# AV of a chunk's second query block as one 128-row matmul per head, in a fused sliding-window attention and SwiGLU kernel

## The chip, the cores and the metric

One Trainium2 chip; the kernel runs on one of its cores. The time is the device time of one execution in microseconds, given as the median of several runs.

## What is computed

```python
# q, k, v: (8, 8, 576, 64) float32;  w_gate, w_val: (512, 1536);  w_out: (1536, 512)
scores = np.matmul(q, k.transpose(0, 1, 3, 2)) / 8.0
mask = (rel >= 0) & (rel < 64)             # rel = query position - key position
attn = softmax(np.where(mask, scores, -1e9))
attn_out = np.matmul(attn, v)              # (8, 8, 576, 64)
x = attn_out.transpose(0, 2, 1, 3).reshape(4608, 512)
g = x @ w_gate
out = (g * sigmoid(g) * (x @ w_val)) @ w_out      # (4608, 512) float32
```

A query sees itself and the 63 positions before it in its own batch. The 4608 tokens are 8 batches of 576.

## The kernel before

The tokens are cut into 36 chunks of 128 (`NCH`), each of two blocks of 64 queries. A query block sees the keys of its own block and of the block before it. Four chunks make one FFN chunk of 512 tokens (`NFC` = 9).

Every step is written by hand, and `_Graph` turns its reads and writes into semaphore waits. Each engine runs its steps in exactly the order in which `build` issues them, so TensorE's order is the order of the calls. The steps that matter here:

- `S(n)` (`Sa`, `Sbias`, `Sb`): scores of chunk n, transposed (keys on partitions). Per pair of heads it issues 64x64 matmuls (lines 394 and 398). ScalarE's Exp writes `pt` (line 406), and VectorE multiplies by the mask (line 409); in the first chunks a matmul with `nmask` (line 374) adds a bias in place of the mask.
- `pt[n]` holds, for each of 8 heads, a 128x128 block. Partitions 0 to 63 are the keys of the chunk's first block, for all 128 queries. Partitions 64 to 127 hold for the first 64 columns (first query block) the keys of the *previous* chunk's last block, and for the last 64 columns (second query block) the keys of the chunk's own second block.
- `AV(n)` (`AVa`, `AVmm`, `AVn`): probabilities times V, with a column of ones in V that gives the sums. `AVmm` runs in two phases of 16 matmuls (line 439), each of 64 rows, 64 columns of weights and 65 moving columns. `r` is the row half of the TensorE array (which keys) and `c` the column half (which query block); in a phase the four matmuls of one `j` go to the four quadrants of the array. The two phases add into the same PSUM, and phase 1 waits for the end of phase 0 by a semaphore (`after=done[0]`). `AVn` divides by the sums on VectorE (lines 454, 457) into `xb`.
- `X(n)`: transposes `xb` into `xT`, by TensorE (line 490) in the first chunks, later by a DMA on SP's queue. `T2` (line 347) transposes k and q of the first chunks on TensorE with 128 rows and 64 columns of weights; later chunks use DMA transposes.
- `F(c, fs)`: gate and value matmuls of an FFN chunk, 128x128 weights and 512 moving columns (256 or 128 in places), 4 per `f` and weight (line 552), then Tanh on ScalarE (line 558) and two VectorE steps (lines 560, 562) into `hT`.
- `O(c, u)`: 12 matmuls of 128x128 weights and 512 columns (line 578), a copy on ScalarE (line 583) and a store on its queue.

`build` first loads (`loads`; on GpSimd's DMA queue, in order of issue), runs dummy matmuls on zeros (`warm`, line 527), then an opening with chunks 0 to 3 in a hand-made order, then chunks 4 to 11 mixed with the F steps of FFN chunks 0 and 1. From FFN chunk 2 on there is a regular stage for each token chunk n:

```python
self.load(n + 4)
self.B(n)          # AVmm(n, 0), S(n + 1), AVmm(n, 1), AVn(n)
self.X(n)
self.Tkq(n + 3)
F(c, (3 * u,)); F(c, (3 * u + 1,)); O(c - 1, u); F(c, (3 * u + 2,))
```

`B` is also what chunks 8 to 11 use; it puts the scores of the next chunk between the two phases of AV.

Of the kernel before, what the change touches and what calls it, by code (L numbers as in the profile page):

```python
# [151 lines left out]
class _Kernel:  # L152
# [181 lines left out]
    def T2(self, st, x, engs):  # L334
        g = self.g
        src = (self.ks2 if x == "k" else self.qs2)[st % 2]
        dst = self.kT if x == "k" else self.qT
        z0 = (2 * st) % self.NZ
        for cc in range(2):
            bank, bk = self.bank("a")  # L340
            tb = bank[:, 0:256].bitcast(BF).rearrange("p (c j t) -> p c j t", c=2, j=2)

            def pe(e, cc=cc, tb=tb):
                for c in range(2):
                    for j in range(2):
                        for p in range(2):
                            r = e.transpose(tb[64 * p:64 * p + 64, c, j, :], src[:, 4 * cc + 2 * c + p, j, :], self.ident[:, :])  # L347
                return r

            g.op("pe", pe, reads=["ident", ("s2", x, st % 2, 0), ("s2", x, st % 2, 1)], writes=[bk])  # L350
            d = dst[:, 2 * cc:2 * cc + 2, 128 * z0:128 * z0 + 256].rearrange("p c (t j) -> p c t j", j=2)
            a = tb.rearrange("p c j t -> p c t j")
            self.copy(engs[cc], d, a, [bk], [(x + "T", z, cc) for z in (z0, z0 + 1)])
# [57 lines left out]
    def S(self, n, bias=False):  # L411
        if n < NCH:
            self.Sb(self.Sa(n, bias))
# [9 lines left out]
    def AVmm(self, st, phase):  # L423
        n, bx, av, done = st
        iv, jv, ip = n % self.NV, (n - 1) % self.NV, n % self.NP
        va, vb, pt = self.va[iv], self.va[jv], self.pt[ip]

        def pe(e):
            for j in range(4):
                for r in range(2):  # L430
                    p = r if phase == 0 else 1 - r
                    h = 2 * j + p
                    for c in range(2):
                        if n == 0 and r == 1 and c == 0:
                            continue
                        first = j == 0 and (phase == 0 or (n == 0 and c == 0 and r == 0))
                        rows = slice(64 * r, 64 * r + 64)
                        vv = vb if (r == 1 and c == 0) else va
                        x = e.matmul(av[64 * c:64 * c + 64, p, j, :], pt[rows, h, 64 * c:64 * c + 64], vv[rows, h, 0:65],  # L439
                                     start=first, stop=phase == 1, skip_group_check=True)  # L440
            return x

        rd = [("pt", ip, 0), ("pt", ip, 1)]
        for i in {iv, jv} if n else {iv}:
            rd += [("va", i), ("va", i, 0), ("va", i, 1)]
        done.append(self.g.op("pe", pe, reads=rd, writes=[b[1] for b in bx], after=done[0] if phase else None))
# [27 lines left out]
    def X(self, n, eng="sp", kind="f"):  # L474
        if n >= NCH:
            return
        g = self.g
        ix, it, u = n % 4, (n // 4) % self.NX, n % 4
        xb = self.xb[ix]
        xo = self.xT[it][:, :, 128 * u:128 * u + 128]  # L480
        xk = [("xb", ix, 0), ("xb", ix, 1)]
        if eng == "sp":
            g.op("sp", lambda e: e.dma_start_transpose(xo, xb[:, :]), reads=xk, writes=[("xT", it, u)], dma=True)
            return
        bank, bk = self.bank(kind)
        tb = bank[:, 0:256].bitcast(BF).rearrange("p (c t) -> p c t", c=4)

        def pe(e):
            for c in range(4):
                r = e.transpose(tb[:, c, :], xb[:, 128 * c:128 * c + 128], self.ident[:, :])  # L490
            return r

        g.op("pe", pe, reads=["ident"] + xk, writes=[bk])
        self.copy(eng, xo, tb, [bk], [("xT", it, u)])
# [122 lines left out]
    def loads(self):  # L617
        self.first_loads()
        self.load2(0, "q")
        self.load2(1, "k")  # L620
        self.load2(1, "q")
        self.init()
        self.init_ident()
        self.init_mask(0)
        self.init_mask(1)
        self.load(0, "v")
        self.load(1, "v")
        self.load_w("g", 0, 2)
        self.load(2, "v")
        self.load(3, "v")  # L630
        self.load_w("v", 0, 2)
        for a in range(2, 10, 2):
            self.W(a, a + 2)

# [21 lines left out]
    def build(self):  # L656
        F, S, AV, X, T2, O = self.F, self.S, self.AV, self.X, self.T2, self.O
        self.loads()
        self.banks("a", [4, 5, 6, 7, 0, 1, 2, 3, 4, 5, 0, 1, 2, 3, 0, 1, 6, 7, 4, 5, 6, 7, 4, 5, 2, 3, 6, 7])
        self.warm(90, n=64)  # L660
        self.first_T(("dve", "act"))
        self.init_nmask()
        self.warm(2)
        s0 = self.Sa(0)
        T2(0, "q", ("act", "dve"))
        self.Sbias(s0)
        self.Sb(s0)
        T2(1, "k", ("dve", "dve"))
        s1 = self.Sa(1, True)
        self.Sb(s1)  # L670
        T2(1, "q", ("dve", "act"))
        self.early_loads()
        s2, s3 = self.Sa(2, True), self.Sa(3)
        a0, a1, a2, a3 = self.AVa(0), self.AVa(1), self.AVa(2), self.AVa(3)
        self.AVmm(a0, 0)
        self.AVmm(a0, 1)
        self.AVn(a0)
        self.Sb(s2)
        self.AVmm(a1, 0)
        self.AVmm(a1, 1)  # L680
        self.AVn(a1)
        self.Sbias(s3)
        X(0, "act", "a")
        self.Sb(s3)
        X(1, "dve", "a")
        self.AVmm(a2, 0)
        self.AVmm(a2, 1)
        self.AVn(a2)
        self.AVmm(a3, 0)
        self.AVmm(a3, 1)  # L690
        self.AVn(a3)
        F(0, (0, 1), 0, 256)
        X(2, "act", "a")
        X(3, "act", "a")
        F(0, (2, 3), 0, 256)
        F(0, (0, 1), 256, 512)
        self.banks("a", [4, 5, 6, 7])
        self.init_va(4, self.NV)
        self.more_loads()
        F(0, (2, 3), 256, 512)  # L700
        F(0, (4, 5), 0, 256)
        F(0, (4, 5), 256, 512)
        F(0, (6, 7), 0, 256)
        F(0, (6, 7), 256, 512)
        T2(2, "k", ("act", "act"))
        T2(2, "q", ("act", "act"))
        F(0, (8, 9), 0, 256)
        S(4)
        F(0, (8, 9), 256, 512)
        S(5)  # L710
        AV(4)
        F(0, (10,), 0, 512)
        AV(5)
        F(0, (11,))
        X(4, "act")
        T2(3, "k", ("act", "act"))
        X(5, "act")
        F(1, (0, 1), 0, 128)
        T2(3, "q", ("act", "act"))
        F(1, (0, 1), 128, 256)  # L720
        S(6)
        F(1, (2, 3), 0, 256)
        S(7)
        AV(6)
        F(1, (4, 5), 0, 256)
        AV(7)
        F(1, (6, 7), 0, 256)
        X(6, "act")
        F(1, (8, 9), 0, 256)
        X(7, "act")  # L730
        for n in (10, 11, 12):
            self.load(n)
        for n in range(8, 12):
            self.Tkq(n)
        F(1, (10, 11), 0, 256)
        S(8)
        F(1, (0, 1), 256, 512)
        O(0, 0)
        self.load(13)
        self.load(14)  # L740
        self.Tkq(12)
        self.B(8)
        X(8)
        self.Tkq(13)
        F(1, (2, 3), 256, 512)
        O(0, 1)
        self.load(15)
        self.B(9)
        X(9)
        self.Tkq(14)  # L750
        F(1, (4, 5), 256, 512)
        F(1, (6, 7), 256, 512)
        self.B(10)
        O(0, 2)
        F(1, (8, 9), 256, 512)
        X(10, "act")
        self.B(11)
        O(0, 3)
        F(1, (10, 11), 256, 512)
        X(11, "act")  # L760
        for c in range(2, NFC):
            for u in range(4):
                n = 4 * c + u + 4
                if n < NCH:
                    self.load(n + 4)
                    self.B(n)
                    self.X(n)
                    self.Tkq(n + 3)
                F(c, (3 * u,))
                F(c, (3 * u + 1,))  # L770
                if n < NCH or u < 3:
                    O(c - 1, u)
                F(c, (3 * u + 2,))
                if n >= NCH and u == 3:
                    O(c - 1, u)
        for u in range(3):
            O(NFC - 1, u)
        self.O_last(NFC - 1, 3)
        self.g.emit()
# [42 lines left out]
```

## Time and profile before

| | us |
|---|---|
| median of 3 runs (lowest, highest) | 338.50 (337.32, 338.95) |
| the profiled execution, its own time | 337.56 |
| its span, first to last instruction | 335.7 |
| TensorE matmuls busy, by the page | 321.4 (96%) |
| VectorE busy | 202.1 (60%) |
| ScalarE busy | 136.2 (41%) |
| GpSimd busy | 105.9 (32%) |

Matmuls overlap in TensorE, so the mean duration of a matmul in the profile is its latency, not the distance to the next one; the distance comes from the starts of neighbouring records. PEld is the loading of weights, with a record of its own for each matmul. Some matmul records are missing from the trace, regularly the first gate matmul after an AV.

### The profile page before, as it was taken

What the parts mean: (1) busy time and instruction counts of PE and PEld (TensorE: products, weight loads), DVE (VectorE), ACT (ScalarE), POOL (GpSimd) and SP (SyncE); (2) the same over time, 40 slices, a digit from 0 to 9 for tenths busy, and PEclk for the clock granted to TensorE, in tenths of its full rate; (3) what the DMA queues carried; (4) which work ended last, traced back from release to release, by engine and by line L of the source; (5) the groups of instructions that cost most, each with busy time, mean ns of one, the idle gap of its engine ahead of it and who ended that gap; (6) DMA issues with size and microseconds to landing.
All of it is one profiled execution on the core that took longest, in us unless ns stands there. A gap on an engine that the chain in (4) does not pass through costs nothing.

```text
span 335.7 us, 8680 instructions
## 1 busy us (share of the span) xinstructions
PE 321.4 (96%) x3734; PEld 177.8 (53%) x3768; DVE 202.1 (60%) x345; ACT 136.2 (41%) x239; POOL 105.9 (32%) x136
## 2 busy tenths in 40 slices
PE   7869999999999999999999999999999999999996
PEld 7558868776544444444444444444444444444444
DVE  3628678657766666666666666666666666555520
ACT  2623665454444444444444443334444442233221
POOL 8999925643514532331432532030000000000000
PEclk9979999999999999999999999999999999999999
DMA  9999999999999999999999999993333311100012
GB/s 141 158 197 185 183 185 151 134 154 159 192 165 172 145 132 115 128 124 128 138 125 120 130 128 119 124 127 81 78 80 80 80 47 49 47 31 34 31 62 94
DMA packets 161574, 39.89 MB, mean 119 GB/s; under 512 B 148608, under 2 KB 157056, under 8 KB 161536
## 3 DMA queue, kind: packets, MB, share of 16 engines
q0 software_dynamic: 111056, 18.62, 81.7%
q1 hardware_dynamic: 45024, 11.15, 25.9%
q10 hardware_dynamic: 5456, 9.57, 8.4%
q8 instruction: 29, 0.48, 0.6%
q14 instruction: 9, 0.07, 0.1%
HBM read 37.75 MB, written 9.44 MB: 141 GB/s over the span
## 4 chain that ended last, share of the span: by engine, by line
PE 74%; ACT 11%; DVE 6%; issue 4%; ACTq 2%; DMA 2%; POOL 1%; POOLq 0%
PE ps L552 42%; PE ps L578 27%; DVE uu L560 5%; ACT ost L583 4%; ACT sig L558 4%; ACTq L585 2%; DMA qs<-in_q_dram 2%; PE ps L439 2%; ACT pt L406 1%; PE ps L600 1%; PE ps L490 1%; PE ps L394 1%; ACT xT L233 1%; PE ps L347 0%; DVE pt L409 0%
## 5 line engine op out<-in xcount | busy, mean ns | idle before, releaser
L560 DVE SCALAR_TENSOR_TENSOR uu<-sig,ps 128x512 bf16<-128x512 bf16 (+1 forms) x109 | 73.8, 677 | 87.8 <-ACT sig L558 87.8
L552 PE MATMUL ps<-xT,Wv 128*128 128x512 bf16 (+2 forms) x526 | 111.8, 342 | 0.1
L552 PE MATMUL ps<-xT,Wg 128*128 128x512 bf16 (+2 forms) x502 | 106.6, 341 | 4.3 <-DVE uu L560 3.9
L578 PE MATMUL ps<-Wo,hT 128*128 128x512 bf16 x415 | 95.0, 379 | 0.5 <-DVE hT L562 0.2
L558 ACT ACTIVATE sig<-ps 128x512 bf16<-128x512 f32 (+1 forms) x109 | 64.8, 595 | 70.1 <-PE ps L552 69.3
L562 DVE SCALAR_TENSOR_TENSOR hT<-uu,ps 128x512 bf16<-128x512 bf16 (+1 forms) x109 | 74.3, 682 | 3.9 <-PE ps L552 0.2
L552 PEld LDWEIGHTS ps<-xT,Wv 128*128 128x128 bf16 x528 | 51.5, 99 | 42.9
L552 PEld LDWEIGHTS ps<-xT,Wg 128*128 128x128 bf16 x528 | 48.4, 98 | 38.7 <-ACT xT L233 0.2
L578 PEld LDWEIGHTS ps<-Wo,hT 128*128 128x128 bf16 x420 | 40.9, 98 | 48.7
L583 ACT ACTIVATE ost<-ps 128x512 f32<-128x512 f32 x35 | 20.9, 597 | 94.4 <-PE ps L578 94.4
L298 POOL DMA_DIRECT2D kn<-in_k_dram x31 | 27.2, 879 | 97.7 <-DMA kT<-kn 96.7
L406 ACT ACTIVATE pt<-ps 128x512 bf16<-128x512 f32 x72 | 39.1, 595 | 20.3 <-PE ps L398 19.1
L298 POOL DMA_DIRECT2D va<-in_v_dram x40 | 35.3, 902 | 6.6 <-PE ps L552 6.0
L409 DVE TENSOR_TENSOR pt<-pt,mask 128x1024 bf16<-128x1024 bf16 x32 | 22.2, 692 | 14.7 <-ACT pt L406 14.7
L298 POOL DMA_DIRECT2D qn<-in_q_dram x31 | 27.4, 888 | 9.0 <-DMA qT<-qn 8.7
L439 PE MATMUL ps<-va,pt 64*64 64x65 bf16 x1144 | 23.2, 197 | 4.3 <-issue 3.5
L457 DVE TENSOR_TENSOR xb<-ps,rc 128x512 bf16<-128x512 f32 x36 | 24.9, 691 | 1.2
L439 PEld LDWEIGHTS ps<-va,pt 64*64 64x64 bf16 x1144 | 15.3, 107 | 17.6 <-issue 14.2
L398 PE MATMUL ps<-qT,kT 64*64 64x64 bf16 x576 | 15.3, 194 | 0.0
L394 PE MATMUL ps<-qT,kT 64*64 64x128 bf16 x288 | 14.3, 217 | 0.3 <-DVE qT L235 0.2
L398 PEld LDWEIGHTS ps<-qT,kT 64*64 64x64 bf16 x576 | 11.8, 108 | 0.0
L394 PEld LDWEIGHTS ps<-qT,kT 64*64 64x64 bf16 x288 | 9.3, 106 | 2.3 <-issue 1.3
(45 smaller groups left out, 84.6 us busy)
## 6 DMA issues: line engine op xcount, KB each, us to landing
out_dram<-ost ACTq DMA_DIRECT2D x35, 256.0 KB, 3.2
va<-in_v_dram POOLq DMA_DIRECT2D x32, 128.0 KB, 11.3
kn<-in_k_dram POOLq DMA_DIRECT2D x25, 128.0 KB, 10.3
qn<-in_q_dram POOLq DMA_DIRECT2D x25, 128.0 KB, 10.0
Wg<-in_moe_w_gate_dram POOLq DMA_DIRECT2D x6, 256.0 KB, 9.0
Wv<-in_moe_w_val_dram POOLq DMA_DIRECT2D x6, 256.0 KB, 9.0
Wo<-in_moe_w_out_dram POOLq DMA_DIRECT2D x2, 768.0 KB, 18.1
qs<-in_q_dram POOLq DMA_DIRECT2D x3, 256.0 KB, 8.0
```

The costliest lines, as they stand in the source:

```text
L298: self.g.op("pool", lambda e, d=d, a=a: e.dma_start(d, a), writes=ks, dma=True)
L394: e.matmul(sv[p][0:64, c, :], self.kT[ps, c, self.zs(n, 0, 64)], self.qT[ps, c, self.zs(n)], **kw)
L398: r = e.matmul(sv[p][64:128, c, a:a + 64], self.kT[ps, c, ks], self.qT[ps, c, self.zs(n, a, a + 64)], **kw)
L406: g.op("act", lambda e, po=po, p=p: e.activation(po, sv[p], ACTF.Exp, scale=SCALE), reads=[bx[p][1]], writes=[pk[p]])
L439: x = e.matmul(av[64 * c:64 * c + 64, p, j, :], pt[rows, h, 64 * c:64 * c + 64], vv[rows, h, 0:65], start=first, stop=phase == 1, skip_gro ...
L457: g.op("dve", lambda e: e.tensor_tensor(xo, av[:, :, :, 0:64], rb, ALU.mult), reads=bk + [("rc", ir)], writes=[("xb", ix, 0), ("xb", ix, 1)])
L552: r = e.matmul(bank[:, a * n:a * n + n], W[:, kk, f * 128:f * 128 + 128], xT[:, kk, lo:hi], start=(kk == 0), stop=(kk == NK - 1))
L558: g.op("act", lambda e, G=bank: e.activation(sig[:, 0:w], G[:, 0:w], ACTF.Tanh, scale=0.5), reads=[bk], writes=[("sig", i)])
L560: g.op("dve", lambda e: e.scalar_tensor_tensor(uu[:, 0:w], sig[:, 0:w], 1.0, G[:, 0:w], ALU.add, ALU.mult), reads=[("sig", i), gk], writes ...
L562: g.op("dve", lambda e: e.scalar_tensor_tensor(out, v3(uu), 0.5, v3(V), ALU.mult, ALU.mult), reads=[("uu", i), vk], writes=[("hT", ih, f) ...
L578: r = e.matmul(OB[:, :], hT[:, f, 128 * u:128 * u + 128], self.Wo[:, f, :], start=(f == 0), stop=(f == NF - 1))
L583: g.op("act", lambda e: e.activation(ost[:, :], OB[:, :], ACTF.Copy), reads=[ok], writes=[("ost", io)])
```

## The change

- In `AVmm`, the second query block (`c` = 1, outputs on partitions 64 to 127) no longer takes two 64-row matmuls that are added over the two phases. Its keys are all in the chunk itself, so one matmul per head with 128 rows, 64 columns of weights and 65 moving columns does it. A phase has four of these, for the heads 2j + phase. The first query block (`c` = 0) stays as it was, two 64-row matmuls per head over the two phases. A phase goes from 16 matmuls to 12, in the order: one of 128 rows, two of 64 rows, four times over. For chunk 0, which has no previous block, it goes from 12 to 8.
- `warm(90, n=64)` becomes `warm(60, n=96)`.
- In `loads`, V of chunk 3 is issued after the first pair of Wv instead of before it.

```diff
         def pe(e):
             for j in range(4):
+                h = 2 * j + phase
+                e.matmul(av[64:128, phase, j, :], pt[:, h, 64:128], va[:, h, 0:65],
+                         start=j == 0, stop=True, skip_group_check=True)
                 for r in range(2):
+                    if n == 0 and r == 1:
+                        continue
                     p = r if phase == 0 else 1 - r
                     h = 2 * j + p
-                    for c in range(2):
-                        if n == 0 and r == 1 and c == 0:
-                            continue
-                        first = j == 0 and (phase == 0 or (n == 0 and c == 0 and r == 0))
-                        rows = slice(64 * r, 64 * r + 64)
-                        vv = vb if (r == 1 and c == 0) else va
-                        x = e.matmul(av[64 * c:64 * c + 64, p, j, :], pt[rows, h, 64 * c:64 * c + 64], vv[rows, h, 0:65],
-                                     start=first, stop=phase == 1, skip_group_check=True)
+                    first = j == 0 and (phase == 0 or n == 0)
+                    rows = slice(64 * r, 64 * r + 64)
+                    x = e.matmul(av[0:64, p, j, :], pt[rows, h, 0:64], (vb if r else va)[rows, h, 0:65],
+                                 start=first, stop=phase == 1, skip_group_check=True)
             return x
...
         self.load(2, "v")
+        self.load_w("v", 0, 2)
         self.load(3, "v")
-        self.load_w("v", 0, 2)
...
-        self.warm(90, n=64)
+        self.warm(60, n=96)
```

## The prediction

> **What bounds the kernel now.** I read the page first, then the chain of waits for one regular stage, then the timeline of TensorE record by record wherever the array changes the shape of its tiles, since that is what the change does most.
>
> ```profile
> span 335.7 us, 8680 instructions
> ## 1 busy us (share of the span) xinstructions
> PE 321.4 (96%) x3734; PEld 177.8 (53%) x3768; DVE 202.1 (60%) x345; ACT 136.2 (41%) x239; POOL 105.9 (32%) x136
> ...
> PEclk9979999999999999999999999999999999999999
> ```
>
> TensorE is busy for 96% of the span and no other engine for more than 60%. In the third slice its clock falls to 0.7. From 24 us on, the distances between matmul records leave almost no wait: a regular stage (gate matmul at 121.58 to the same one at 130.10) takes 8.52 us. Its 36 wide matmuls start 216 ns apart and make 7.78 of it; the other 0.74 is AV, the scores, and the changes between them and the wide ones. So each nanosecond that AV adds on TensorE in a stage is a nanosecond of the whole.
>
> ```profile
> 128.26 1.03 PE L552 MATMUL ps<-xT,Wv 128*128 128x512 bf16 x4
> 129.22 0.32 PE L439 MATMUL ps<-va,pt 64*64 64x65 bf16 x16
> ...
> 129.57 0.23 PE L398 MATMUL ps<-qT,kT 64*64 64x64 bf16 x4
> 129.62 0.32 PE L439 MATMUL ps<-va,pt 64*64 64x65 bf16 x16
> 130.10 0.38 PE L552 MATMUL ps<-xT,Wg 128*128 128x512 bf16 x1 [0.16 <-DVE uu L560]
> ```
>
> This is AV of one stage (start, extent, tile shape as rows*columns). Sixteen matmuls of a phase fill four quadrants at once: their records start in groups of four, 3 ns apart, a group every 20 to 43 ns, and the last starts 128 ns after the first. The scores follow 20 ns later, and phase 1 follows the scores 17 ns later: all are 64*64. But from the last wide matmul (128.912) to the first of AV (129.221) there are 309 ns, against 216 between wide ones. The 0.16 us of waiting in the last line is a missing record; the weights for it load at 129.87.
>
> **What a change of tile shape costs.** Distance from the last matmul of one shape to the first of the next, when nothing else is waited for: 309 ns after 512 columns, 202 after 256, 149 to 152 after 128, 123 to 125 after 64 or 65. Within a shape those columns take 216, 109, 56 and about 30 ns. So each change adds 93 to 98 ns, whatever the two shapes, in every pair that occurs. The pair that counts occurs once without another wait, from the scores to the transposes of `T2`:
>
> ```profile
> 9.34 0.22 PE L394 MATMUL ps<-qT,kT 64*64 64x128 bf16 x2
> 9.36 0.23 PE L398 MATMUL ps<-qT,kT 64*64 64x64 bf16 x4
> 9.52 0.47 PE L347 MATMUL ps<-ident,ks 128*64 128x128 bf16 x10
> ```
>
> Last 64*64 start 9.396, first 128*64 start 9.519: 123 ns. The first transpose goes to the left half of the array; the last two scores (lines 398) were in the right half. In the left half the last were the two at 9.336 and 9.339, of 128 columns, done by 9.392; 96 ns after that is 9.488. The transpose came at 9.519, which is the last score's 27 ns of streaming and 96 ns more. So the array waited for a matmul in a half that the new one does not use: the emptying is of the whole array. The Trainium skill, "TensorEngine Tiling (Array Packing)", section Key Properties, says the same of any change of mode, and lists 128×64 and 64×64 as two configurations; it covers the direction 128*64 to 64*64, which no row here shows. I bound that direction by the rows 128*64 to 128*128 (152 ns after 128 columns) and 64*64 to 128*128 (124 after 65), which give the same 96.
>
> **AV, part by part.** The new phase is A (128*64), B, C (64*64), four times, so it changes shape seven times inside. Low bound: 124 ns each, as above. But there the last matmul before the change had its weights loaded ahead. Right after a change they are not: the weight load starts with the matmul, and the record is longer, 214 ns against 189 to 193 (lines 439 at 129.221 and 129.274). A next shape has always started 66 to 70 ns before that recorded end (193 and 123, 219 and 152, 379 and 309). In the new phase each of A, B and C is the first after a change, so I take 214 − 68 = 146 ns. First start to last start of a phase: 4 × (146 + 3) + 3 × 146 = 1034 ns (low bound 4 × 127 + 3 × 123 = 877) in place of 128: +906 ns (low +749).
>
> - Chunks 4 to 35, two phases each: 64 × 0.906 = 58.0 us (low 47.9).
> - In `B` phase 1 now follows the scores with a change of shape, 123 ns for 17: 27 chunks (8 to 34) × 0.106 = 2.9. AV(4) and AV(6) also follow scores: 0.2. Without scores between, phase 1 starts about 260 ns after phase 0's last start because of the semaphore, which covers the change: 0.
> - Out of AV into the wide matmuls: a change before as after, 146 for 124: 32 × 0.022 = 0.7.
> - The four fewer matmuls per phase save nothing: they ran 3 ns beside others.
>
> Sum 61.8 (low 51.0), all on TensorE's path: from 24 us on, waits inside it beyond changes of shape are at most about 0.2 us each, and the only regular one (phase 0 to phase 1) is counted above.
>
> **The opening (chunks 0 to 3).** Here there is a wait, and it takes part of it.
>
> ```profile
> 15.25 0.72 PE L439 MATMUL ps<-va,pt 64*64 64x65 bf16 x32
> 19.49 0.83 PE L439 MATMUL ps<-va,pt 64*64 64x65 bf16 x32 [3.52 <-issue]
> 20.25 1.89 PE L552 MATMUL ps<-xT,Wg 128*128 128x256 bf16 x8
> ...
> 19.90:23.10 3.20, 3.20 (x30) 2.34 (x31) 1.19 (x3) 0.60 (x1) 3.20 (x5) 0.50 1.45 196
> ```
>
> AV(3) starts at 19.49 although its `pt` is ready at 16.23 and its V is seen by TensorE at 15.71; a 16 KB packet on the instruction queue begins at 17.14, so late instructions are my guess. After this the clock is 0.50 until 23.2 (the line of the windows), and 16 matmuls of 256 columns take 3.18 us where 16 × 0.109 = 1.75 would do. With the long AVs I step through TensorE's order: AV(0) 12.32 to 14.65, S(2), AV(1) 15.05 to 17.40, bias, X(0), S(3) to 18.57, X(1), AV(2) 19.0 to 21.35, AV(3) 21.5 to 23.85, first gate matmul at 24.0 for 20.25: +3.75. AV(3) now comes after 19.49, with no wait before it, so the clock should stay up: −1.43. Together +2.3 (low, with 124 ns: first gate at 22.6, +0.9; high: the clock falls nevertheless, +3.8).
>
> **The other two edits.** The dummies start 53 ns apart at 64 columns, 1.2 columns per ns as at the clock of 0.50; 60 × 96 are the same 5760 columns and end at the same 6.1. The next matmul waits for VectorE's cast until 6.69, so up to 0.5 us is hidden; if they ended early at the load rate (60 × 53 ns, at 4.5), the bound is the clock rising one 3.4 us period later, some 1.5 us. V of chunk 3 goes one GpSimd issue later (0.81 us) and behind Wv's 512-byte packets, which took about 1.4 us; its landing at 15.45 becomes at most 17.7, and AV(3) is at 21.5: 0. Wv comes earlier, first needed at 25. If AV were short, the cover would be 19.49 − 17.7.
>
> **Sum.** 337.56 (the profiled execution: 335.7 and 1.9 around it) + 61.8 + 2.3 = 401.7; the low bound 337.56 + 51.0 + 0.9 = 389.5. The profiled execution is 0.9 under the median of the runs, inside their 1.6 us of spread; I take 402.
>
> **Rivals.**
>
> *No emptying between 128*64 and 64*64: faster.* A lies in the right half, B and C in the left, so no quadrant is shared inside a phase. Then each `j` takes about 30 ns as now. The change has 60 + 64 fewer matmuls before AV(3) ends, twice that in instructions; if the wait at 15.8 is for instructions, it goes, with the half clock: 337.56 − 3.3 − 1.4 = 332.9. If the wait stays, 337 to 338. For it: distinct tiles do run at 3 ns here. Against: 9.519. It decides if a pair A, B starts under about 50 ns apart. The Trainium skill, "TensorE: Matmul & The Clock Gate", section Part 3, speaks for this side: tiles of different row groups overlap, with about 4 ns for each, so by it alone a phase would span some 40 ns above one matmul and the time would be about 333. Chance 0.10 (0.07 under −0.5%, 0.03 within 0.5%).
>
> *Only the way into 128*64 empties.* Half the changes inside: 62 → about 31, 370 us. Against: every pair seen costs the same both ways. Chance 0.04.
>
> *The clock falls in the regular stages.* AV and scores now take about 2.6 us at low activity; the stall above shows a fall after 3.5 us of idling. A 3.4 us period at half clock in each of 28 stages costs up to 28 × 1.4 = 39: 440. Against: the clock held from 12.3 to 16.4, with waits and little streaming. The Trainium skill, "TensorE: Matmul & The Clock Gate", Part 1, asks for a whole idle window of about 3.4 us, which would leave the clock at full and this rival at nothing. Chance 0.05.
>
> **How the numbers follow.** Emptying both ways: 0.81, at 402. Its own range is 388 to 407: the low bound of 389.5 less the 1.2 us that runs lie below their median; 402 with the high opening (+1.5), the dummies' bound (+1.5) and 148 ns per change (+0.9), and a little of the same spread. That holds perhaps nine in ten of the 0.81, so for 8 in 10 the range goes on on both sides, toward the cases at 370 and 440: 382 to 411. About 0.5% (1.7 us) is what a measurement of this kernel can tell from no change: faster 0.07, same 0.03, slower 0.90.
>
> **What would show it.** Right: a regular stage of about 10.4 us (8.52 + 1.81 + 0.13); first to last start of a phase about 1.03 us, with 140 to 148 ns per change; first gate matmul near 24 us at full clock; wide matmuls still 216 ns apart. At 10.1 us a stage, the weights' share is wrong. A stage near 8.5 us makes the prediction wrong, and A and B 3 ns apart shows why.

## Result and the profile after

| | before | after |
|---|---|---|
| median of 6 runs each, us | 338.1 (337.32 to 339.4) | 411.06 (405.57 to 413.04) |
| ratio, 95% interval | | 1.2097 [1.2017, 1.2176] |
| profiled execution, us | 337.56 | 408.70 |
| its span, us | 335.7 | 406.9 |
| its mean TensorE clock | 0.995 | 0.975 |

The change makes the kernel 21% slower. The forecast was 402, with a range up to 411: the direction and the mechanism hold, and the median lies 9 us above the forecast, at the upper end of the range (0.06 beyond it). The ratio leaves out the two runs that lie more than 1.5% above the fastest (411.89 and 413.04), so it is a little under 411.06 / 338.1.

The page of the changed kernel:

```profile
span 406.9 us, 8044 instructions
...
PE 396.6 (97%) x3416; PEld 227.6 (56%) x3450; DVE 207.8 (51%) x345; ACT 136.7 (34%) x239; POOL 106.0 (26%) x136
...
PEclk9759999899999999999999999999999999899999
```

TensorE is still the bound, now with fewer instructions in a longer span. The busy share says nothing here: it is 97% with an array that is emptied again and again. The clock row shows what I had not put into the sum: a dip early (slices 2 and 3), and two short ones later (slices 8 and 35).

The timeline of TensorE in a regular stage (start, extent, tile shape rows*columns):

```profile
151.47 0.22 PE L431 MATMUL ps<-va,pt 128*64 128x65 bf16 x1
151.62 0.22 PE L440 MATMUL ps<-va,pt 64*64 64x65 bf16 x2
151.77 0.22 PE L431 MATMUL ps<-va,pt 128*64 128x65 bf16 x1
151.92 0.22 PE L440 MATMUL ps<-va,pt 64*64 64x65 bf16 x2
...
152.51 0.22 PE L440 MATMUL ps<-va,pt 64*64 64x65 bf16 x2
...
152.89 0.22 PE L431 MATMUL ps<-va,pt 128*64 128x65 bf16 x1
...
153.92 0.22 PE L440 MATMUL ps<-va,pt 64*64 64x65 bf16 x2
154.30 0.38 PE L553 MATMUL ps<-xT,Wg 128*128 128x512 bf16 x1 [0.16 <-issue]
```

Each 128-row matmul is alone, and each pair of 64-row ones stands about 0.15 us behind it, although the two use different halves of the array. Record by record the way from 128*64 to 64*64 takes 148 ns (288 times, median) and the way back 144 (226 times). A phase is 1036 ns long from first to last start, where it was 128. The stage is 10.47 us, where it was 8.52.

The windows of the same execution (stretch, length, busy time of each engine with instructions, then TensorE's clock, DMA share, GB/s):

```profile
12.20:15.60 3.40, 3.34 (x49) 2.42 (x48) 0.90 (x2) 1.15 (x3) 3.40 (x5) 1.00 1.71 164
15.70:29.20 13.50, 13.31 (x110) 8.63 (x111) 3.37 (x8) 2.39 (x5) 13.50 (x19) 0.50 1.54 191
29.30:70.20 40.90, 40.43 (x505) 31.75 (x504) 27.01 (x50) 18.53 (x35) 24.84 (x31) 1.00 1.86 166
66.90:70.10 3.20, 3.14 (x32) 2.19 (x30) 1.76 (x4) 0.01 (x1) 1.49 (x3) 1.00 2.01 153
70.30:73.50 3.20, 3.20 (x19) 2.34 (x18) 1.69 (x3) 1.05 (x2) 2.27 (x3) 0.50 1.78 155
```

In the opening the clock is at half from 15.6 to 29.3 us, where before it was at half for 3.4 us. It falls again for 3.4 us at 70.2 and at 353.5. Busy time does not show why: TensorE is "busy" for 3.34 of 3.40 us ahead of the first fall.

### The profile page after: what moved, and what is told of

It is laid out like the page before. It is cut to its first block, busy times and chain, and to the rows that moved or that the text cites. A ratio compares the mean times of both kernels' runs of the same rounds, so it can differ in the third digit from the quotient of the medians.

```text
span 406.9 us, 8044 instructions
## 1 busy us (share of the span) xinstructions
PE 396.6 (97%) x3416; PEld 227.6 (56%) x3450; DVE 207.8 (51%) x345; ACT 136.7 (34%) x239; POOL 106.0 (26%) x136
## 4 chain that ended last, share of the span: by engine, by line
PE 95%; issue 1%; DMA 1%; ACT 1%; DVE 1%
PE ps L553 46%; PE ps L579 22%; PE ps L431 11%; PE ps L440 11%; PE ps L394 1%; DMA hT<-in_k_dram 1%; PE ps L398 1%; PE ps L491 1%; PE ps L347 1%; PE ps L601 1%; PE ps L374 1%; ACT pt L406 0%; ACT xT L233 0%; ACT qT L233 0%; ACT kT L233 0%
## 5 line engine op out<-in xcount | busy, mean ns | idle before, releaser
L553 PE MATMUL ps<-xT,Wv 128*128 128x512 bf16 (+2 forms) x526 | 113.5, 346 | 0.1
L553 PE MATMUL ps<-xT,Wg 128*128 128x512 bf16 (+2 forms) x502 | 108.2, 345 | 4.0 <-issue 3.8
L431 PE MATMUL ps<-va,pt 128*64 128x65 bf16 x288 | 63.6, 221 | 0.6
L440 PE MATMUL ps<-va,pt 64*64 64x65 bf16 x568 | 63.5, 217 | 0.0
L431 PEld LDWEIGHTS ps<-va,pt 128*64 128x64 bf16 x288 | 31.0, 108 | 24.4 <-issue 12.1
L440 PEld LDWEIGHTS ps<-va,pt 64*64 64x64 bf16 x568 | 31.0, 104 | 12.3
L455 DVE RECIPROCAL rc<-ps 128x8 f32<-128x8 f32 x36 | 7.3, 202 | 15.0 <-PE ps L440 15.0
```

Source lines behind the costliest of these rows:

```text
L431: e.matmul(av[64:128, phase, j, :], pt[:, h, 64:128], va[:, h, 0:65], start=j == 0, stop=True, skip_group_check=True)
L440: x = e.matmul(av[0:64, p, j, :], pt[rows, h, 0:64], (vb if r else va)[rows, h, 0:65], start=first, stop=phase == 1, skip_group_check=True)
L553: r = e.matmul(bank[:, a * n:a * n + n], W[:, kk, f * 128:f * 128 + 128], xT[:, kk, lo:hi], start=(kk == 0), stop=(kk == NK - 1))
```

## Experiments

The theory: the array empties at each change of tile shape, whatever halves are in use; that is seven changes inside a phase and one ahead of phase 1. Rivals: the 128-row matmul itself is slow; the small edits have a part in it; the clock is what costs the time.

### The same matmuls in another order

In short (A: a matmul of 128 rows; BC: the two 64-row matmuls of one `j`):

```diff
-  order in a phase: A0 BC0 A1 BC1 A2 BC2 A3 BC3
+  one change:       A0 A1 A2 A3 BC0 BC1 BC2 BC3
+  three changes:    A0 A1 BC0 BC1 A2 A3 BC2 BC3
```

One change inside a phase, expected: 

> The changed kernel with the same matmuls in another order: in each phase first the four of 128 rows, then the eight of 64 rows. One change of tile shape inside a phase where there were seven. If the changes of shape cost the time, first to last start of a phase falls from 1.03 us to about 0.31 (97 for the four, 124 for the change, 90 for the four pairs): 64 x 0.72 = 46 us off, the opening's 6 us too, and no fall of the clock: 345 to 356. If the 128-row matmuls themselves are slow (a row half of another size, weights of 128 rows), the order does not matter and it stays at 400 or more. If tiles of different columns needed only the same order to overlap, it would be near 338.

Three changes, expected: 

> As the kernel with one change of shape per phase, but in two groups: two of 128 rows, four of 64, two of 128, four of 64; three changes inside a phase. If the cost is a fixed amount per change, a phase takes about 0.55 us, and the time is about a third of the way from the kernel with one change to that with seven: 364 to 372. If the cost comes with the first departure from 64x64 alone, or with each 128-row matmul, it is the same as with one change.

| changes inside a phase | phase, ns | median, us | ratio to before, interval |
|---|---|---|---|
| 0 (before: all 64*64) | 128 | 337.69 | |
| 1 | 363 | 351.90 | 1.0403 [1.0343, 1.0463] |
| 3 | 594 | 368.63 | 1.0895 [1.0841, 1.0950] |
| 7 (the change) | 1036 | 411.06 | 1.2097 [1.2017, 1.2176] |

TensorE in a stage of the kernel with one change:

```profile
151.49 0.31 PE L431 MATMUL ps<-va,pt 128*64 128x65 bf16 x4
151.73 0.25 PE L442 MATMUL ps<-va,pt 64*64 64x65 bf16 x4
...
152.20 0.31 PE L431 MATMUL ps<-va,pt 128*64 128x65 bf16 x4
152.44 0.31 PE L442 MATMUL ps<-va,pt 64*64 64x65 bf16 x8
```

The four 128-row matmuls follow each other 52, 36 and 30 ns apart: they are not slow. Each further change adds (594 − 363) / 2 = 116 ns and then (1036 − 594) / 4 = 111 ns to a phase. The order alone is worth 59 us, so this is shown: the loss is in the number of changes. Of the 59 us, 72 phases × 0.673 = 48.5 us are the changes themselves. The rest fits the clock, which follows from them: it is at half for 20.5 us of the changed kernel, which costs at most 10.2, and it stays up to the last 0.1 us of the kernel with one change. From one change to three, where the clock stays up too, the same count gives 72 × 0.231 = 16.6 us, and 16.7 are measured. Both expectations held for the time; my phases were 52 and 44 ns short, since four matmuls in the same half take 118 ns to the last start and not 97, and four pairs of 64-row ones about 120 and not 90.

A change takes 123 to 127 ns in these two kernels against 144 to 148 in the changed one, and the weight loads show the difference: the load of the last matmul ahead of a change starts 24 to 29 ns before that matmul here, and 0 to 3 ns before it in the changed kernel.

### The two small edits alone, and the AV alone

```diff
 e1_small_edits = before, with
-        self.warm(90, n=64)
+        self.warm(60, n=96)
 and load(3, "v") behind load_w("v", 0, 2);   e2_av_alone = before, with the new AVmm only
```

Small edits alone, expected: 

> The kernel before with the two small edits alone (60 dummies of 96 columns; V of chunk 3 behind the first Wv pair), AV as before. If the AV matmuls carry the whole loss, this is the kernel before within 1.5 us: 336.5 to 339. If the small edits had a part in it, by a later V or a later rise of the clock, it is slower by 1.5 us or more. If the wait ahead of AV(3) is for TensorE's instructions, it comes 60 instructions later in the program (inside AV(3), not ahead of it) and is about as long.

AV alone, expected: 

> The kernel before with the new AV alone; dummies and the order of the V load as before. If the AV carries the whole loss, it is the changed kernel again: 405 to 413, with a phase of 1.03 us and a fall of the clock in the opening. If the two small edits, which alone cost 2.9 us, cost as much beside the new AV, it is 3 us faster than the changed kernel: 405 to 410 with a median near 408. The long AVs come to AV(3) after V of chunk 3 has landed, so I expect no difference that can be told.

AV alone: 409.28 us (ratio 1.2136 [1.2077, 1.2196]), the same as the whole change. The small edits alone: 340.56 against 337.69, ratio 1.0075 [1.004, 1.011]. So they do cost, which I had not expected, but only where AV is short. TensorE in the opening with the small edits alone:

```profile
15.95 0.72 PE L439 MATMUL ps<-va,pt 64*64 64x65 bf16 x32
18.16 0.70 PE L439 MATMUL ps<-va,pt 64*64 64x65 bf16 x30 [1.49 <-DMA va<-in_v_dram]
20.86 0.26 PE L439 MATMUL ps<-va,pt 64*64 64x65 bf16 x2 [2.00 <-issue]
21.05 0.40 PE L552 MATMUL ps<-xT,Wg 128*128 128x256 bf16 x1
```

AV(3) waits for V of chunk 3 until 18.16. Then it stops once more, after 30 of its 32 matmuls. Before, the stop was just ahead of AV(3): it moved by 30 matmuls with their weight loads, which is 60 instructions, as many as the dummies lost. In both traces 695 records of matmuls and weight loads stand ahead of it. The wait ends 2.28 us after a packet on the instruction queue (18.58), as before it ended 2.35 us after one (17.14). So the wait ahead of AV(3) is for TensorE's instructions. After it the clock is at half for 6.8 us in place of 3.4. In the changed kernel AV(3) starts at 23.2 and neither wait is there.

### Fewer dummy instructions in the kernel before

```diff
-        self.warm(90, n=64)
+        self.warm(11, n=512)
```

Expected: 

> The kernel before with its 90 dummies of 64 columns as 11 of 512: nearly the same columns, 158 TensorE instructions fewer (a weight load goes with each). If the wait of 3.5 us ahead of AV(3) is for instructions, TensorE now comes to the same count of instructions some 5 us later, inside the first FFN steps, where it uses them slower than they arrive: the wait and the half clock after it go, 3.3 + 1.4 us, so 333 to 334.5. If the wait is for data or for ScalarE, it stays at 19.5 us and the time is 337.5 to 339.

336.47 us, ratio 0.9969 [0.9934, 1.0004]: not told from no change, and over the 333 to 334.5 that I expected. The opening of this kernel:

```profile
15.98 0.72 PE L439 MATMUL ps<-va,pt 64*64 64x65 bf16 x32
16.91 0.72 PE L439 MATMUL ps<-va,pt 64*64 64x65 bf16 x32 [0.22 <-ACT pt L406]
17.56 1.05 PE L552 MATMUL ps<-xT,Wg 128*128 128x256 bf16 x8
```

The wait and the half clock are gone as expected, the first gate matmul comes at 17.56 for 20.25, and from 38 to 55 us the kernel is 4.0 us ahead. Between 72 and 87 us it gives 2.7 us of that back, most of it in one wait of 1.8 us at 84.2. I tried to take that wait away by two transposes on TensorE:

```diff
         self.B(8)
-        X(8)
+        X(8, "act")          # and X(9) alike; in the second try one F step later
```

Right behind B, expected: 

> The kernel before with 11 dummies of 512 columns, and X(8) and X(9) by TensorE in place of a DMA transpose on SP's queue. With 11 dummies alone the kernel is 4.0 us ahead at 60 us, and gives 2.7 us of it back between 72 and 87, 1.8 us of that in one wait of a gate matmul at 86.2. If that wait is for the DMA transpose of X(9), it goes here: 334.5 to 335.5, about 1% under the kernel before. If it is for the keys and queries of the next chunks, the time stays at 336 to 337, plus 0.3 for the eight transposes.

One FFN step later, expected: 

> The kernel before with 11 dummies of 512 columns, and X(8) and X(9) by TensorE, each one FFN step later in TensorE's order than in the last try (behind F(1, (2, 3), 256, 512) and F(1, (4, 5), 256, 512)). There TensorE stood 3.6 and 3.3 us for the division of AV ahead of these transposes; an FFN step of 1.75 us and more lies between now. If the wait at 84.2 to 86.0 us of the kernel with 11 dummies is for the two DMA transposes on SP's queue, it goes, and the time is 334 to 335.5, 1% under the kernel before. If the keys and queries of later chunks pace that stretch, it stays at 336 to 337.5.

Both are misses: 344.99 us (1.0216 [1.0162, 1.0270]) and 339.28 (1.0024 [0.9990, 1.0057]). The waits of the first one (total, how often, the longest):

```profile
PEld ps L490 <- DVE xb L457: 6.8, 2, 3.6
PE ps L490 <- DVE xb L457: 6.6, 2, 3.5
```

TensorE runs in program order, so a transpose in it makes everything behind it wait for the division of AV on VectorE: 3.6 and 3.3 us, and still 1.8 and 1.4 one step later. In the first try the clock also falls to half for 3.4 us behind each of the two waits (at 65.5 and 75.7). With the transpose on the DMA queue TensorE does not stand for that division. What paces the stretch from 72 to 87 us stays open, and no version beats the kernel before clearly.

### The clock

From the records I worked out for each 3.41 us period (aligned to the recorded changes of the clock) the share of time in which any matmul streams columns. A column takes 0.417 ns at full clock, from the distances of wide matmuls with 512 and with 128 columns, (216 − 56) / 384, and twice that at half; overlaps are counted once, and a wide matmul whose record is missing is counted in:

| kernel | period, us | share | clock after it |
|---|---|---|---|
| before | 16.37 to 19.79 | 0.04 | 0.5 |
| before, next lowest | 12.96 to 16.37 | 0.54 | 1.0 |
| after | 12.19 to 15.61 | 0.24 | 0.5 |
| after | 66.81 to 70.22 | 0.368 | 0.5 |
| after | 350.11 to 353.52 | 0.370 | 0.5 |
| after, lowest without a fall | 213.58 to 216.99 | 0.412 | 1.0 |
| AV alone | 48.20 to 51.61 | 0.34 | 0.5 |
| AV alone | 68.68 to 72.09 | 0.371 | 0.5 |
| AV alone, lowest without a fall | 351.98 to 355.39 | 0.374 | 1.0 |

Falls and holds part at about 0.37, and the other kept traces agree: none falls after a period with more, none holds after one with less. Counting each matmul by the part of the array that it uses does not part them (a hold at 0.29 in the kernel with three changes, falls at 0.30 in the changed kernel). The return of the clock fits the same count. At half, a column takes twice the time, so 0.37 at full clock is 0.74 at half; the clock stayed down after periods with 0.28 to 0.70 of streaming and rose after 0.77 or more.

Behind the opening, the falls come at particular places. In the three traces of kernels with the full change or the AV alone (the changed kernel, AV alone, and the one with fillers below) there are five: at AV(4), AV(5), twice AV(7), and AV(35). In these the two phases stand without scores between them, as here in AV(35), the last one of the changed kernel:

```profile
351.29 0.22 PE L431 MATMUL ps<-va,pt 128*64 128x65 bf16 x1
351.44 0.22 PE L440 MATMUL ps<-va,pt 64*64 64x65 bf16 x2
351.72 0.22 PE L431 MATMUL ps<-va,pt 128*64 128x65 bf16 x1
```

The scores between the phases of AV(8) to AV(34) keep the share at 0.41 or more, however the period lies over them, and none of these 27 stages falls in any of the three traces.

To test the share I put streaming into the opening, and nothing else:

```diff
         self.AVmm(a0, 0)
+        self.fill(4)          # four dummies of 512 columns; behind each AV phase of chunks 0 to 3
         self.AVmm(a0, 1)
+        self.fill(4)
```

Expected: 

> The changed kernel with four dummy matmuls of 512 columns behind each of the eight AV phases of the opening (chunks 0 to 3), nothing else. They add work: 8 x 4 x 0.216 = 6.9 us at full clock, and a change of shape each. If the clock falls because too small a share of a 3.41 us period is streaming (falls so far at 0.37 and less, none at 0.41 and more), the share here is about 0.5, the clock stays at 1.0 through the opening, and the first gate matmul comes at about 31.5 at full clock: the time is only about 4 us above the changed kernel, 409 to 416. If the clock falls for another reason (the many changes of shape, or the time since the start), it falls here too, and the opening takes 12 us or more in addition: over 418.

The opening of the kernel with the fillers, first the window, then the timeline:

```profile
10.00:31.00 21.00, 20.47 (x230) 11.94 (x229) 5.75 (x12) 5.12 (x10) 21.00 (x28) 1.00 1.58 181
```

```profile
30.21 1.04 PE L538 MATMUL ps<-wz 128*128 128x512 bf16 x3
31.08 1.04 PE L563 MATMUL ps<-xT,Wg 128*128 128x256 bf16 x8
31.96 1.04 PE L563 MATMUL ps<-xT,Wv 128*128 128x256 bf16 x8
```

The clock stays at 1.00 through the opening, where the periods that it fills now have shares of 0.49 to 0.62, and the first gate matmul comes at 31.08. With 6.9 us of added work the 17th gate or value matmul of 256 columns is only 3.3 us later than in the changed kernel (33.28 for 29.98), and the time is 411.14 (two runs) against 411.06. In this execution one fall remains, after the period 54.91 to 58.32 with 0.371. So the time since the start does not lower the clock. The fillers also leave fewer changes of shape in each period, but it fell as well in the kernel before, where TensorE only waited (0.04), and behind the two waits of the transposes (0.15 and 0.12). What all these periods share is the small part of streaming, not the changes as such.

## Why the prediction was right, and where it was short

- **A change of shape empties the whole array, both ways.** This held, with the right size: 146 ns forecast, 148 and 144 measured; a phase of 1034 forecast, 1036 measured; into phase 1 behind the scores 123 forecast, 123 measured. The rival without emptying (333) fell with the first pair of records, 148 ns apart; so did the one that empties one way only (370). The count under the first rival was off: the change has 30 dummies and 32 AV matmuls fewer up to the end of AV(3), 62 together, and 60 + 64 are the instructions, weight loads included. No time rests on it.
- **The regular part.** Forecast 61.8 us. Measured: the last matmul starts 71.15 us later, the 17th gate or value matmul 6.10 us later, so 65.1 us between. The two falls of the clock in it take at most 2 × 1.7 us, which leaves 61.7. The stage of "about 10.4 us" is 10.47.
- **The opening is the term that was mis-sized.** Forecast +2.3, with a high end of +3.8; measured +6.1 (the first gate matmul comes at 26.4, not at 24.0). I had written that, with no wait ahead of AV(3), "the clock should stay up". It fell at 15.6, in the middle of the long AVs, and stayed down for 13.65 us. My reason was that the clock had held from 12.3 to 16.4 "with waits and little streaming". The share there was 0.54; with the new AV it is 0.24. I should have worked the share out for both, from the same records.
- **The rival of the clock in the regular stages** was wrong in place and size; what it had right is that a period over an AV can fall with TensorE never idle. I had it fall in each stage at 1.4 us, or never. In the regular stages it never fell, since the scores between the phases keep the share at 0.41 or more. It fell at AV(7) and AV(35), which have no scores there, and cost at most 3.4 us, a term that the sum had at nothing. With the 3.8 us of the opening this makes up the 7.0 us between 401.7 and the profiled 408.70.
- **The spread of the runs** goes with the clock: the six runs have mean clocks from 0.963 to 0.983 and spans from 411.2 to 403.7, and span times clock lies between 395.6 and 397.4 in all six. 2 × (1 − clock) × span gives 14 to 30 us at half clock, four to nine periods, four of which the opening takes in the profiled run. At which places the runs without a trace lose the others is not shown.
- **The two small edits at nothing.** This held inside this change: with the AV alone the time is the same. The cover I named (AV(3) at 21.5 us) is what hides them; without it they cost 0.75%, and V landed for TensorE at 18.16 and not by 17.7.
- **The wait for instructions**, a guess in the prediction, is shown by the run with the small edits. That it goes was right, but it earns nothing here: with the AV alone, and none of the dummies taken away, the wait is gone as well.

## What to carry to other kernels

Count the changes of tile shape in TensorE's order, not its matmuls: here each costs 111 to 116 ns net, about four times what a group of small matmuls takes, and from first to last start 12 matmuls in mixed shapes took eight times as long as 16 in one. If two shapes are needed, put all of one shape first; the order alone was worth 59 us here. Before trusting the clock, work out the share of a 3.4 us period in which columns really stream: the busy share of the page counts the emptying as work.

## What the runs showed that I had not expected

- The clock falls without idling. The Trainium skill, "TensorE: Matmul & The Clock Gate", Part 1, ties the fall in its table of states to an idle window of about 3.4 us, and tells of one kernel whose short idles did it too, without a measure; here it fell after periods with 0.24 to 0.37 of streaming and no wait of TensorE longer than 0.3 us in the first of them. The length of the period agrees: all falls last 3.41 us or a multiple.
- The clock can stay down for four periods although matmuls go on all the time (15.61 to 29.26): at half clock they have to fill about three quarters of a period, and the long AVs fill 0.28 to 0.56.
- In the opening TensorE ran out of instructions: a wait of 3.5 us that moved by exactly the 60 instructions taken away ahead of it, and went when 158 were taken away. Each matmul, however small, takes two: itself and its weight load.
